# A recurrent attention and two expert layers on one core: the u, k, r diagonal of the first eight units formed in unit layout

## The chip, the core and the metric

The program runs on one core of one Trainium2 chip. The metric is the device time of one execution in microseconds; the three runs of the kernel before took 944.08, 945.52 and 947.94 us.

## What is computed

```
# r, k, v, w: [4, 8, 768, 48] (batch, head, token, channel); u: [8, 48]
for t in range(768):
    cur = einsum('bhd,bhe->bhde', u * k_t, v_t)
    y_t = einsum('bhd,bhde->bhe', r_t, state + cur)
    state = w_t[..., None] * state + einsum('bhd,bhe->bhde', k_t, v_t)
x = y as [3072, 384]
h = x @ w_in;  x = (max(h, 0) + alpha * min(h, 0)) @ w_out     # d_ff = 2048
h = x @ w2_in; out = (h * clip(h + 3, 0, 6) / 6) @ w2_out
```

The change touches one term: the share of a token in its own output, which is the sum over the channels of u, k and r, times v. It stands on the diagonal of a 128 x 128 matrix of weights between tokens.

## The kernel before, in words

**Units.** Each of the four batches of 768 tokens is cut into thirds of 256 tokens (12 thirds t), and the eight heads into four pairs, so there are 48 units n = 4t + pair. A unit's load `un` (L368) holds k, r and w of 256 tokens with 48 channels of one head on partitions 0 to 47 and of the other on 64 to 111. DVE makes two scans of products of w (scan_t L386, scan_g L402, with two small steps between, L394 and L399), POOL or DVE multiplies k and r by them (kr, L423), and PE multiplies k by r for two chunks of 128 tokens and two heads into `A` (function pa, L477) and transposes k (L484). ACT copies that transpose to `kT` (L509), PE multiplies it by v (KV, L516 and L520), DVE carries the state Y on, and ACT spreads Y into block matrices (state, L538).

**The diagonal.** X is a tile of four 128 x 128 matrices, one per head and chunk. ACT writes each as the identity times one number per partition (diag, L458, four activations), and DVE then copies the upper triangle of A over it (triangle, L494 or L499). X and the state matrices give the output y on PE (pc, L588 to L599). ACT writes its upper part (L635, the tile xt, or x for the fourth pair), DVE the rest (L641). The fourth pair's x goes out by six small transfers on SP (spread, L651).

**Where the numbers of the diagonal come from.** They are formed per third in token layout: `add_third` loads for each of two chunks r and k with tokens on partitions (rk, L328), multiplies them by one another and by u_sb (L332, two products, POOL or DVE), and sums them over the channels of each head on DVE (L339) into `p`. u_sb is loaded at the start (L292).

**The experts.** Both layers go by 6 blocks of 512 tokens and 16 slots of 128 columns. A slot is nine matmuls into h (L765 to L767), an activation and a product that split the result in two parts, and nine matmuls into three accumulators. Weight tiles come as 64-bit words (wraw, L729) and pass ACT (L95), DVE (L98, L103), ACT (L738) and DVE or POOL (L742).

**What sets the order.** Class `Plan` (L117) takes every step with the engines that it may run on, a cost for each, a due time and its dependencies, simulates a list schedule by these costs, and the program is then written out engine by engine in the resulting order. Each engine runs its instructions strictly in that order. SP issues all loads and stores. Steps that are marked `pair` are kept from running on POOL and DVE at the same time. Before the first expert matmul the planner fills PE with warming matmuls (L682). Units 0 to 7 are `early`: they use tiles that the experts need later, and every second one has its A in two banks of the accumulators; the others share one A.

Of the kernel before, what the change touches and what calls it, by code (L numbers as in the profile page):

```python
# [7 lines left out]
F32 = mybir.dt.float32  # L8
# [6 lines left out]
AF = mybir.ActivationFunctionType  # L15
ALU = mybir.AluOpType
# [4 lines left out]
P = 128  # L21
B, H, S, D = 4, 8, 768, 48
NPAIR = 4
C = 128
TH = 256
NTH = 12
NT = B * S
DM = H * D
# [3 lines left out]
PR = 112  # L32
# [6 lines left out]
AHEAD = 8  # L39
# [6 lines left out]
def rwkv_moe_moe2(  # L46
# [13 lines left out]
    nc = tc.nc  # L60
    keep = ctx.enter_context(tc.tile_pool(name="keep", bufs=1))
    dram = ctx.enter_context(tc.tile_pool(name="dram", bufs=1, space=DRAM))
    flag = keep.tile([1, 1], I32, name="flag")
    alp = keep.tile([P, NF], F32, name="alp")
    x2d = dram.tile([NB, NK, P, TB], F32, name="x2d")

    with ExitStack() as es:
        fast_path(es, tc, unit, tok, vch, ub, w1, w2, alpha, out, flag, alp, x2d)
# [161 lines left out]
def fast_path(es, tc, unit, tok, vch, ub, w1, w2, alpha, out, flag, alp, x2d):  # L230
    nc = tc.nc
# [18 lines left out]
    u_sb = const.tile([P, DM], F32, name="u_sb")  # L250
    nal = const.tile([P, NF], F32, name="nal")
# [11 lines left out]
    def setup():  # L263
# [8 lines left out]
        nc.vector.memset(ones, 1.0)  # L272
        nc.vector.memset(three, 3.0)
# [18 lines left out]
    o_u = plan.op({"SP": 0.6}, -38.5, lambda e: nc.sync.dma_start(u_sb, ub))  # L292
# [18 lines left out]
    def add_third(t):  # L311
# [7 lines left out]
        v_op[t] = plan.op({"SP": 1.12}, due + 2, load_v, new=[vb]), vb  # L319
        pb = plan.buf("p", 2)  # L320
# [33 lines left out]
    def add_unit(n):  # L354
# [6 lines left out]
        vb, (reds, pb) = v_op[t][1], p_op[t]  # L361
# [91 lines left out]
        def diag(e):  # L453
            pool, tag, nb = (mp, "g", 3) if early else (ap_, "X", 2)
            X = u["X"] = pool.tile([P, 4, C], F32, tag=tag, bufs=nb, name=f"X{n}")
            pp = p_t[t][:, pr].rearrange("p h c -> p (h c)")
            for i in range(4):
                nc.scalar.activation(X[:, i], ident, AF.Copy, scale=pp[:, i : i + 1])  # L458

        o_x = plan.op({"ACT": 1.18}, d - 1, diag, reds, new=[xb], use=[pb])  # L460
# [4 lines left out]
        def pa(e):  # L465
# [17 lines left out]
            for c in range(nkv):  # L483
                nc.tensor.transpose(  # L484
                    T[:, c, :], kr[:, 0, c * C : (c + 1) * C], ident[0:PR, 0:PR]
                )

        o_pa = plan.op({"PE": 0.89 + 0.1 * nkv}, d - 2, pa, o_kr, new=abufs, use=[krb])
# [18 lines left out]
        def kt(e):  # L507
            u["kT"] = ap_.tile([P, 2, PR], F32, tag="kT", bufs=2, name=f"kT{n}")
            nc.scalar.activation(u["kT"][:, 0:nkv, :], u["Tp"][:, 0:nkv, :], AF.Copy)  # L509

        o_kt = plan.op({"ACT": 0.26}, d + 0.5, kt, [o_pa], new=[ktb], use=abufs)
# [684 lines left out]
```

## Time and profile before

| what | us |
|---|---|
| median of 3 runs | 945.52 |
| lowest, highest | 944.08, 947.94 |
| the profiled execution | 945.74 |
| its span, first to last instruction | 944.0 |
| PE busy | 920.3 (97%) |
| DVE busy | 556.3 (59%) |
| ACT busy | 530.9 (56%) |
| POOL busy | 132.3 (14%) |

The busy share is an average over the whole span. The program has a start, in which the early units run and the first weights are prepared, a middle, in which units and slots alternate, and a long end of slots alone; what a microsecond of an engine is worth differs between them, so the stretches have to be read apart. A row of the trace gives the start and the length of an instruction, or of several merged ones with their count; records of neighbouring instructions of an engine may overlap a little.

### The profile page before, as it was taken

The page shows a single profiled execution, that of the slowest core. Times are in us where ns is not written, and L with a number is a line of the kernel's source. Part 1 is how long each engine was busy: PE and PEld are TensorE (multiplying, and loading weights), DVE is VectorE, ACT ScalarE, POOL GpSimd, SP SyncE. Part 2 cuts the span into 40 slices and gives each one's busy share as a digit, 9 for nine tenths or more (in the row PEclk, how much of TensorE's full clock was granted, in tenths as well). Part 3 has the DMA queues.
Part 4 walks back from the last instruction along what each step waited for, and adds up shares of the span by engine and source line. Part 5 has one row for each costly group of instructions (what it writes and reads, how often), then busy time and mean ns, then how long its engine had stood idle before and what let it go on. Part 6 is the DMA issues. An engine that isn't in the chain of part 4 may idle for free.

```text
span 944.0 us, 13745 instructions
## 1 busy us (share of the span) xinstructions
PE 920.3 (97%) x4914; PEld 743.2 (79%) x4914; DVE 556.3 (59%) x1087; ACT 530.9 (56%) x1266; POOL 132.3 (14%) x132
## 2 busy tenths in 40 slices
PE   7899989999999999999999999999999999999996
PEld 5677767878888788878888888888888888888885
DVE  8999997465655645564369886353353443443432
ACT  5998776565656655665378876363353453443331
POOL 4333234021121201100011130000000000000000
PEclk9999999999999999999999999999999999999998
DMA  8888214122312310110056530060140320500001
GB/s 250 256 268 283 81 52 145 55 79 70 107 64 57 109 55 31 58 64 7 9 186 197 175 111 1 1 200 1 54 147 1 123 79 1 172 30 1 34 1 38
DMA packets 36750, 86.20 MB, mean 91 GB/s; under 512 B 5056, under 2 KB 7488, under 8 KB 36672
## 3 DMA queue, kind: packets, MB, share of 16 engines
q1 hardware_dynamic: 36672, 85.22, 28.8%
q8 instruction: 41, 0.67, 0.3%
q14 instruction: 37, 0.30, 0.1%
HBM read 73.41 MB, written 9.44 MB: 88 GB/s over the span
## 4 chain that ended last, share of the span: by engine, by line
PE 82%; DVE 1%; DMA 0%; POOL 0%; issue 0%; POOLq 0%; DVEq 0%
PE acc L765 13%; PE acc L767 13%; PE acc L766 13%; PE h L765 12%; PE h L767 12%; PE h L766 12%; PE A L477 2%; PE y L595 1%; PE y L588 1%; PE A L484 1%; DMA rk<-in_tok 0%; PE y L599 0%; PE A L516 0%; POOL rk L332 0%; PE A L520 0%; DVE rk L332 0%
## 5 line engine op out<-in xcount | busy, mean ns | idle before, releaser
L765 PE MATMUL acc<-g,w 128*128 128x512 f32 x576 | 228.9, 397 | 0.0
L767 PE MATMUL acc<-g,w 128*128 128x512 f32 x576 | 224.6, 390 | 0.0
L766 PE MATMUL acc<-g,w 128*128 128x512 f32 x576 | 224.5, 390 | 0.0
L818 ACT ACTIVATE g<-pg 128x512 fp32r<-128x512 f32 x192 | 120.6, 628 | 137.7 <-PE acc L767 126.8
L821 DVE TENSOR_TENSOR g<-pg,g 128x512 fp32r<-128x512 f32 x176 | 121.7, 691 | 124.8 <-ACT g L818 124.7
L765 PEld LDWEIGHTS acc<-g,w 128*128 128x128 f32 x576 | 108.1, 188 | 23.4 <-issue 0.4
L767 PEld LDWEIGHTS acc<-g,w 128*128 128x128 f32 x576 | 108.1, 188 | 22.8
L766 PEld LDWEIGHTS acc<-g,w 128*128 128x128 f32 x576 | 108.2, 188 | 21.6 <-DVE g L821 0.3
L812 DVE SCALAR_TENSOR_TENSOR pg<-q,h 128x512 f32<-128x512 f32 x96 | 65.9, 686 | 98.6 <-ACT q L803 98.4
L808 DVE SCALAR_TENSOR_TENSOR pg<-h,q 128x512 f32<-128x512 f32 x96 | 66.1, 688 | 96.4 <-ACT q L801 96.3
L803 ACT ACTIVATE q<-h,three 128x512 f32<-128x512 f32 x96 | 65.8, 685 | 100.5 <-PE h L767 100.3
L765 PE MATMUL h<-xt,w 128*128 128x512 f32 x288 | 116.3, 404 | 1.2 <-ACT w L738 1.1
L767 PE MATMUL h<-xt,w 128*128 128x512 f32 x288 | 113.0, 392 | 0.9 <-POOL w L742 0.7
L766 PE MATMUL h<-xt,w 128*128 128x512 f32 x288 | 112.3, 390 | 0.0
L765 PE MATMUL h<-x,w 128*128 128x512 f32 x288 | 112.0, 389 | 0.0
L766 PE MATMUL h<-x,w 128*128 128x512 f32 x288 | 112.0, 389 | 0.0
L767 PE MATMUL h<-x,w 128*128 128x512 f32 x288 | 112.0, 389 | 0.0
L801 ACT ACTIVATE q<-h,nal 128x512 f32<-128x512 f32 x96 | 65.6, 684 | 73.6 <-PE h L767 71.7
L423 POOL TENSOR_TENSOR kr<-un,tg 112x512 f32<-112x512 f32 (+1 forms) x43 | 43.6, 1016 | 225.5 <-PE y L588 207.3
L765 PEld LDWEIGHTS h<-xt,w 128*128 128x128 f32 x288 | 54.9, 191 | 13.3 <-ACT w L738 2.2
L767 PEld LDWEIGHTS h<-xt,w 128*128 128x128 f32 x288 | 54.0, 188 | 14.1 <-DVE w L742 1.4
L766 PEld LDWEIGHTS h<-x,w 128*128 128x128 f32 x288 | 54.1, 188 | 11.3
(93 smaller groups left out, 1262.7 us busy)
## 6 DMA issues: line engine op xcount, KB each, us to landing
wraw<-in_w SPq DMA_DIRECT2D x64, 384.0 KB, 3.7
un<-in_unit SPq DMA_DIRECT2D x48, 337.3 KB, 3.2
raw<-in_w SPq DMA_DIRECT2D x32, 384.0 KB, 3.9
rk<-in_tok SPq DMA_DIRECT2D x24, 384.0 KB, 4.0
v<-in_vch SPq DMA_DIRECT2D x12, 384.0 KB, 3.1
x2d<-st SPq DMA_DIRECT2D x18, 256.0 KB, 2.1
x2r<-x2d SPq DMA_DIRECT2D x18, 256.0 KB, 4.6
out<-st SPq DMA_DIRECT2D x18, 256.0 KB, 3.5
```

The lines of the kernel that those rows point to most:

```text
L423: eng[e].tensor_tensor(out=u["kr"][:, i].rearrange("p a (c s) -> p a c s", c=2), in0=u["in"][:, 0 : 2 * TH].rearrange("p (a c s) -> p a c ...
L477: nc.tensor.matmul(A[h][:, cs], kr[r0 : r0 + D, 0, cs], kr[r0 : r0 + D, 1, cs], start=True, stop=True,)
L484: nc.tensor.transpose(T[:, c, :], kr[:, 0, c * C : (c + 1) * C], ident[0:PR, 0:PR])
L765: nc.tensor.matmul(ps, whi, xhi, start=start, stop=False, skip_group_check=True)
L766: nc.tensor.matmul(ps, whi, xlo, start=False, stop=False, skip_group_check=True)
L767: nc.tensor.matmul(ps, wlo, xhi, start=False, stop=stop, skip_group_check=True)
L801: nc.scalar.activation(q, k["h"], AF.Relu, scale=nal[:, f : f + 1])
L803: nc.scalar.activation(q, k["h"], AF.Relu, bias=three)
L808: nc.vector.scalar_tensor_tensor(out=p, in0=k["h"], scalar=0.0, in1=k["q"], op0=ALU.max, op1=ALU.subtract)
L812: nc.vector.scalar_tensor_tensor(out=p, in0=k["q"], scalar=6.0, in1=k["h"], op0=ALU.min, op1=ALU.mult)
L818: nc.scalar.activation(k["g"][:, 0], k["p"], AF.Copy)
L821: eng[e].tensor_tensor(out=k["g"][:, 1], in0=k["p"], in1=k["g"][:, 0].bitcast(F32), op=ALU.subtract)
```

## The change

For t = 0 and 1 (units 0 to 7) `add_third` returns after the load of v: no token loads, products or sums. Instead each early unit forms z = k u r in its own layout, by one scalar_tensor_tensor on DVE over 256 columns (weigh), with u as one number per partition (a new tile udt of 112 x 4, loaded first). In pa two matmuls more multiply z, chunk by chunk, by a matrix `heads` of 112 x 2 with ones at the rows of each head; their four result columns lie behind the transposes in A. ACT's copy of kT takes these four columns along (228 columns for 224), and diag reads its scales from there, so it now comes after kT of its own unit. The z tiles use the buffers `rk`. The load of u_sb gets a later due time. From t = 2 on all is as before.

```
@@ setup and first loads @@
+        nc.vector.memset(heads, 0.0)
+        nc.vector.memset(heads[0:64, 0:1], 1.0)
+        nc.vector.memset(heads[64:PR, 1:2], 1.0)
...
-    o_u = plan.op({"SP": 0.6}, -38.5, lambda e: nc.sync.dma_start(u_sb, ub))
+    o_ud = plan.op({"SP": 0.5}, -44.0, lambda e: nc.sync.dma_start(udt, ud))
+    o_u = plan.op({"SP": 0.6}, -12.0, lambda e: nc.sync.dma_start(u_sb, ub))
...
@@ add_third @@
         v_op[t] = plan.op({"SP": 1.12}, due + 2, load_v, new=[vb]), vb
+        if t < AHEAD // NPAIR:
+            return
...
@@ add_unit @@
-            pp = p_t[t][:, pr].rearrange("p h c -> p (h c)")
+            if early:
+                pp = u["p"].rearrange("p (c h) -> p h c", h=2)
+            else:
+                pp = p_t[t][:, pr]
             for i in range(4):
-                nc.scalar.activation(X[:, i], ident, AF.Copy, scale=pp[:, i : i + 1])
-
-        o_x = plan.op({"ACT": 1.18}, d - 1, diag, reds, new=[xb], use=[pb])
+                h, c = divmod(i, 2)
+                nc.scalar.activation(X[:, i], ident, AF.Copy, scale=pp[:, h, c : c + 1])
+
+        def weigh(e):
+            z = ap_.tile([P, 2, DM], F32, tag="rk", bufs=2, name=f"z{n}")
+            u["z"] = z[0:PR, 0, 0:TH]
+            eng[e].scalar_tensor_tensor(
+                out=u["z"], in0=u["in"][:, 0:TH], scalar=udt[:, pr : pr + 1],
+                in1=u["in"][:, TH : 2 * TH], op0=ALU.mult, op1=ALU.mult,
+            )
+
+        if early:
+            zb = plan.buf("rk", 2)
+            o_z = plan.op(
+                {"DVE": 0.35}, d - 2, weigh, [o_load, o_ud], new=[zb], use=[ub_], pair=True
+            )
+            o_kr.append(o_z)
+        else:
+            reds, pb = p_op[t]
+            o_x = plan.op({"ACT": 1.18}, d - 1, diag, reds, new=[xb], use=[pb])
...
+            if early:
+                for c in range(2):
+                    nc.tensor.matmul(
+                        A[0][:, 2 * (C + PR + c) : 2 * (C + PR + c + 1)],
+                        u["z"][:, c * C : (c + 1) * C], heads, start=True, stop=True,
+                    )
...
+            t2 = ap_.tile([P, 2 * PR + 4], F32, tag="kT", bufs=2, name=f"kT{n}")
+            u["kT"] = t2[:, 0 : 2 * PR].rearrange("p (c d) -> p c d", c=2)
+            u["p"] = t2[:, 2 * PR :]
+            m = 2 * PR + 4 if early else nkv * PR
+            nc.scalar.activation(t2[:, 0:m], u["Ah"][0][:, 2 * C : 2 * C + m], AF.Copy)
...
+            {"ACT": 0.26}, d - 1.2 if early else d + 0.5, kt, [o_pa], new=[ktb], use=abufs
+        if early:
+            o_x = plan.op({"ACT": 1.18}, d - 1, diag, [o_kt], new=[xb], use=[ktb])
```

The planner makes a new order of it. A row below gives the line, the operation, what is written and read (the number behind a name counts tiles) and the shape. First SP, the start of its queue, before (un are unit loads, rk token loads, v the values):

```order
L368 DMA un_142<-in_unit 112x771
L328 DMA rk_147<-in_tok 128x768
L292 DMA u_sb<-in_ub 128x384
L328 DMA rk_158<-in_tok 128x768
L317 DMA v_172<-in_vch 128x768
L368 DMA un_181<-in_unit 112x771
L368 DMA un_197<-in_unit 112x771
L368 DMA un_200<-in_unit 112x771
L328 DMA rk_207<-in_tok 128x768
L328 DMA rk_229<-in_tok 128x768
L317 DMA v_255<-in_vch 128x768
```

and with the change (udt is the new tile, alp is alpha, wraw a weight tile):

```order
L376 DMA un_147<-in_unit 112x771
L297 DMA udt<-in_ud 112x4
L323 DMA v_156<-in_vch 128x768
L376 DMA un_163<-in_unit 112x771
L376 DMA un_175<-in_unit 112x771
L323 DMA v_186<-in_vch 128x768
L376 DMA un_197<-in_unit 112x771
L299 DMA alp<-in_alpha 128x16
L298 DMA u_sb<-in_ub 128x384
L773 DMA wraw_0_0_221<-in_w 128x384
```

All four token loads are gone, units 1 and 2 follow directly on the first v, and u_sb stands behind unit 3. Next ACT from its second check on, before (junk is the check of a unit's load, X a unit's diagonal, sbd a state step, xt an output):

```order
L446 ACTIVATE junk,sum_w<-un_142 112x259
L509 ACTIVATE kT_204<-A_187 128x224
L446 ACTIVATE junk,sum_w<-un_181 112x259
L458 ACTIVATE X_216<-ident,p_194 128x128 x4
L538 ACTIVATE sbd_103<-Y_0_226,tg_162 48x48 x2
L458 ACTIVATE X_249<-ident,p_194 128x128 x4
L458 ACTIVATE X_275<-ident,p_194 128x128 x4
L635 ACTIVATE xt_294,sum_y<-y_264 112x256
L509 ACTIVATE kT_307<-A_0_282 128x224
L446 ACTIVATE junk,sum_w<-un_197 112x259
L458 ACTIVATE X_314<-ident,p_194 128x128 x4
```

and with the change:

```order
L454 ACTIVATE junk,sum_w<-un_163 112x259
L454 ACTIVATE junk,sum_w<-un_175 112x259
L549 ACTIVATE kT_237<-A_199 128x228
L454 ACTIVATE junk,sum_w<-un_197 112x259
L470 ACTIVATE X_245<-ident,kT_237 128x128 x4
L95 ACTIVATE wa_109<-wraw_0_0_221 128x384
L549 ACTIVATE kT_271<-A_0_227 128x228
L582 ACTIVATE sbd_105<-Y_0_274,tg_167 48x48 x2
L470 ACTIVATE X_289<-ident,kT_271 128x128 x4
```

The first three diagonals stood ahead of the second unit's kT; now each stands behind its own unit's kT, the first also behind the check of the fourth unit, and a weight step (wa) comes between the first two units. Last PE around the first expert matmul h, before:

```order
L588 MATMUL y_841<-kr_737,sbd_104 112x128
L588 MATMUL y_841<-kr_737,sbd_105 112x128
L595 MATMUL y_841<-X_677,v_492 48x128
L599 MATMUL y_841<-X_677,v_492 48x128
L595 MATMUL y_841<-X_677,v_492 48x128
L599 MATMUL y_841<-X_677,v_492 48x128
L477 MATMUL A_851<-kr_833 128x128 x4
L484 MATMUL A_851<-ident,kr_833 128x112
L765 MATMUL h_869<-xt_294,w_0_0_673 128x512
```

and with the change, where eight warming matmuls and h follow on the last row:

```order
L505 MATMUL A_787<-kr_762 128x128 x4
L512 MATMUL A_787<-ident,kr_762 128x112
L632 MATMUL y_798<-kr_565,sbd_104 112x128
L632 MATMUL y_798<-kr_565,sbd_105 112x128
L639 MATMUL y_798<-X_743,v_530 48x128
L643 MATMUL y_798<-X_743,v_530 48x128
L639 MATMUL y_798<-X_743,v_530 48x128
L643 MATMUL y_798<-X_743,v_530 48x128
L560 MATMUL A_787<-v_530,kT_808 64x48
L564 MATMUL A_787<-v_530,kT_808 48x48
```

Before, y_841 is the output of unit 9 and A_851 belongs to unit 10; now A_787 belongs to unit 9 and y_798 is the output of unit 8. A of unit 10 and the output of unit 9 follow on the first h. On DVE, from unit 1's scan to x of unit 7, the order has two token products, two sums, two kr of 512 columns, one triangle of 512 columns and one weight product less, and seven z more. On SP the token loads of t = 2 now stand behind the six transfers of unit 3's x, with the loads of units 9 to 11 behind them.

## Rows read from the trace of the kernel before

**Rows 1.** The page, the span in 40 slices of 23.6 us.
```profile
PE   7899989999999999999999999999999999999996
...
DVE  8999997465655645564369886353353443443432
```
**Rows 2.** Busy time by stretches: length, engines (instructions), PEclk, DMA share, GB/s.
```profile
3.00:12.00 9.00, 6.78 (x45) 4.57 (x43) 6.12 (x15) 3.27 (x9) 2.09 (x4) 0.87 1.00 289
11.30:46.00 34.70, 29.02 (x307) 21.75 (x304) 34.46 (x91) 31.76 (x114) 13.67 (x17) 0.97 0.83 252
53.20:160.00 106.80, 101.69 (x597) 76.96 (x595) 99.91 (x205) 83.45 (x219) 35.31 (x31) 1.00 0.55 174
200.00:400.00 200.00, 200.00 (x1220) 160.73 (x1219) 114.18 (x238) 116.36 (x311) 34.41 (x31) 1.00 0.22 68
```
**Rows 3.** Timeline, the end of the start, DVE, SP and PE: start, length, instruction.
```profile
46.99 0.40 DVE L641 TENSOR_TENSOR x<-y,x 112x256 fp32r<-112x256 f32 x1
...
47.42 4.66 SPq L651 DMA_DIRECT2D xt<-x  x6
...
47.23 0.72 PE L477 MATMUL A<-kr 48*128 48x128 f32 x8 [0.20 <-DVE X L499]
...
49.22 0.26 PE L516 MATMUL A<-v,kT 128*64 128x48 f32 x1
...
53.26 0.48 PE L765 MATMUL h<-xt,w 128*128 128x512 f32 x1
```
**Rows 4.** Whom PE waited for, 47 to 200 us: total, times, longest.
```profile
PE A L477 <- DVE fall L394: 1.3, 1, 1.3
PE A L477 <- DVE kr L423: 1.2, 2, 1.0
```
**Rows 5.** Timeline of the start, DVE and ACT; in brackets the idle time before.
```profile
3.93 0.70 DVE L386 TENSOR_TENSOR_SCAN tg<-un,restart 112x258 f32<-112x258 f32 x1 [0.79 <-DMA un<-in_unit]
...
10.82 0.70 DVE L386 TENSOR_TENSOR_SCAN tg<-un,restart 112x258 f32<-112x258 f32 x1 [0.59 <-DMA un<-in_unit]
...
11.30 1.26 ACT L458 ACTIVATE X<-ident,p 128x128 f32<-128x128 f32 x4
...
12.47 0.66 ACT L538 ACTIVATE sbd<-Y,tg 48x48 f32<-48x48 f32 x2
...
45.58 0.38 ACT L635 ACTIVATE x<-y 112x256 fp32r<-112x256 f32 x1
```
**Rows 6.** ACT's groups from 11.25 to 46 us: count, busy us, mean ns, idle before.
```profile
L446 ACT ACTIVATE junk<-un 112x259 bf16<-112x259 f32 x9 | 3.8, 419 | 3.0 <-DMA un<-in_unit 2.9
L95 ACT ACTIVATE wa<-wraw 128x384 uint16<-128x384 uint32 x4 | 2.5, 626 | 0.0
```
**Rows 7.** The tile rk up to 25 us, DVE's sums and products: ns shortest, median, longest.
```profile
L339 DVE TENSOR_REDUCE p<-rk x4: 538/548/553, 7.4 to 22.9; 128x8 f32<-128x384 f32 x4
...
L332 DVE TENSOR_TENSOR rk<-rk x3: 526/541/544, 5.8 to 18.6; 128x384 f32<-128x384 f32 x3
```
**Rows 8.** DVE, timeline at 6.28, then groups from 10.8 to 47.2 us.
```profile
6.28 0.41 DVE L423 TENSOR_TENSOR kr<-un,tg 112x256 f32<-112x256 f32 x1
...
L499 DVE COPY_PREDICATED X<-mask,A 128x512 f32<-128x512 uint8 x5 | 3.6, 722 | 0.0
...
L423 DVE TENSOR_TENSOR kr<-un,tg 112x512 f32<-112x512 f32 x2 | 2.2, 1082 | 0.0
...
L98 DVE SCALAR_TENSOR_TENSOR wb<-wraw,wa 128x384 int32<-128x384 int32 x2 | 1.1, 546 | 0.0
```
**Rows 9.** Whom PE waited for in the whole span: total, times, longest.
```profile
PE A L477 <- DVE kr L423: 4.9, 6, 1.4
```
**Rows 10.** Timeline from 22.2 to 23.4 us, POOL and DVE.
```profile
22.30 0.63 POOL L423 TENSOR_TENSOR kr<-un,tg 112x256 f32<-112x256 f32 x1 [1.13 <-PE A L484]
...
22.40 0.56 DVE L394 TENSOR_SCALAR fall<-tg 112x2 f32<-112x2 f32 x1
...
23.34 0.15 DVE L399 RECIPROCAL gfirst<-fall 112x2 f32<-112x2 f32 x1
```

More of the change, by code (lines that the diff above doesn't have):

```diff
@@ L67, in rwkv_moe_moe2 @@
     with ExitStack() as es:
-        fast_path(es, tc, unit, tok, vch, ub, w1, w2, alpha, out, flag, alp, x2d)
+        fast_path(es, tc, unit, tok, vch, ub, ud, w1, w2, alpha, out, flag, alp, x2d)
     again = nc.values_load(
@@ L227, in run, with fast_path @@
         return seq
-def fast_path(es, tc, unit, tok, vch, ub, w1, w2, alpha, out, flag, alp, x2d):
+def fast_path(es, tc, unit, tok, vch, ub, ud, w1, w2, alpha, out, flag, alp, x2d):
     nc = tc.nc
@@ L250, in fast_path @@
     u_sb = const.tile([P, DM], F32, name="u_sb")
+    udt = const.tile([PR, NPAIR], F32, name="udt")
+    heads = const.tile([PR, 2], F32, name="heads")
     nal = const.tile([P, NF], F32, name="nal")
@@ L360, in add_unit @@
         u = {}
-        vb, (reds, pb) = v_op[t][1], p_op[t]
+        vb = v_op[t][1]
         c0 = pr * 2 * D
@@ L486, in pa @@
                 )
-        o_pa = plan.op({"PE": 0.89 + 0.1 * nkv}, d - 2, pa, o_kr, new=abufs, use=[krb])
+            if early:
[4 more added lines that the diff above has]
+                    )
+        o_pa = plan.op(
+            {"PE": 0.89 + 0.1 * nkv + (0.2 if early else 0.0)}, d - 2, pa, o_kr, new=abufs,
+            use=[krb] + ([zb] if early else []),
+        )
         def triangle(e):
@@ L507, in kt @@
         def kt(e):
-            u["kT"] = ap_.tile([P, 2, PR], F32, tag="kT", bufs=2, name=f"kT{n}")
-            nc.scalar.activation(u["kT"][:, 0:nkv, :], u["Tp"][:, 0:nkv, :], AF.Copy)
-        o_kt = plan.op({"ACT": 0.26}, d + 0.5, kt, [o_pa], new=[ktb], use=abufs)
+            t2 = ap_.tile([P, 2 * PR + 4], F32, tag="kT", bufs=2, name=f"kT{n}")
[3 more added lines that the diff above has]
+            nc.scalar.activation(t2[:, 0:m], u["Ah"][0][:, 2 * C : 2 * C + m], AF.Copy)
+        o_kt = plan.op(
+            {"ACT": 0.26}, d - 1.2 if early else d + 0.5, kt, [o_pa], new=[ktb], use=abufs
+        )
+        if early:
+            o_x = plan.op({"ACT": 1.18}, d - 1, diag, [o_kt], new=[xb], use=[ktb])
         def kv(e):
```

## Prediction

> **What bounds the kernel now.** The page comes first [rows 1]. Its slices show PE at 8 or 9 from the second slice nearly to the end, while DVE stands at 8 or 9 in the first six slices, for three slices near the middle, and otherwise mostly between 3 and 6. The table by stretches gives it in numbers [rows 2]: from 200 to 400 us PE is busy for all 200.00 us, DVE for 114.18. So from there on the end is set by the columns that PE still has to stream, and nothing that gets faster on another engine moves it. What can move it is the start. The first expert matmul begins at 53.26 us [rows 3]; until then PE runs only attention units, each cut up by waits, and 128 warming matmuls that compute nothing. From 53.20 to 160 us PE is busy for 101.69 of 106.80 us [rows 2]; 2.5 us of the waits there are for kr or the small steps of a unit on DVE [rows 4]. I therefore reckon the time as the start of the first h, plus the PE work still owed at that point, plus PE's waits after it.
>
> The start has a chain of its own [rows 3]. DVE writes unit 7's lower half x at 46.99; its six spreading transfers are issued from 47.42 on and hold SP for 4.66 us; 1.2 us after the last issue h begins. These 6.3 us from x to h are not touched. Ahead of x two engines are nearly full: between 11.30 and 46.00 us DVE is busy 34.46 and ACT 31.76 of 34.70 us [rows 2]. Before that neither is: from 3 to 12 us DVE is busy 6.12 and ACT 3.27 of 9.00 us, and the DMA engines are busy throughout at 289 GB/s. So the change has to be costed in two steps, loads first, then ACT and DVE.
>
> **The loads.** Unit 1's scan_t starts at 10.82 us, when its load has landed [rows 5]. Until then the queue has carried units 0 and 1 (0.345 MB each), two token tiles and v (0.393 each) and u_sb (0.197), by their shapes in four-byte numbers: 2.07 MB. In the new SP order only unit 0, 112 x 4 numbers and v stand ahead of unit 1, 1.08 MB with itself. 0.98 MB at 289 GB/s is 3.4 us, so unit 1 can start near 7.4. That is the largest thing the change gives, but ACT does not get it. In ACT's new order the check of unit 3's load stands ahead of the first diagonal. Unit 3 has to wait for the third unit buffer, that is for unit 0's last product. This began at 6.28 on DVE behind a token product [rows 8]; z takes about the place of that, and on POOL the product takes 0.63 [rows 10], so it ends near 6.9. Up to its end 2.17 MB are carried, 0.1 more than up to unit 1 before, so it lands near 11.1, and after the check the first diagonal starts at about 11.5, against 11.30 [rows 5]. It takes 1.26, to 12.8. The next row of ACT is the first step on weight tile 0_0, which has alp and u_sb ahead of it in the queue: 0.6 MB more, 13.2 us. ACT thus stands for 0.4, and begins its full stretch **0.6 us later**, not 3.4 earlier.
>
> **ACT's work up to unit 7's output.** From the first diagonal to the activation that writes x (45.58, [rows 5]) ACT ran 10 diagonals, 13 state steps, 8 checks and 3 first weight steps, besides 8 kT, 8 outputs and 2 weight copies. In the new order it is 8, 14, 6 and 4; the rest is alike. At 1.26 us for a diagonal of four activations, 0.66 for a state step of two, 0.42 for a check (the reading of its accumulator lies under the next) and 0.63 for a weight step [rows 5, 6] this is -2.5 + 0.7 - 0.8 + 0.6 = **-2.0 us**. The diagonals of units 8 and 9 leave the stretch but come later. With the 0.6 of above, unit 7's output and so the first h come **1.4 us earlier**, near 51.9. A kT copy has 4 columns more for 224: nothing.
>
> **DVE's work.** Removed in the first two thirds are 5 products and 4 sums on DVE, 5 x 0.54 + 4 x 0.55 = 4.9 us [rows 7], and 3 products on POOL. Added are 8 z on DVE. The trace has no such form; its bounds are a product of two 112x256 tiles, 0.41 where nothing holds it up, and the integer form with the same three operands on 384 columns, 0.55 [rows 8]. I take 0.41, which has z's columns: DVE saves 4.9 - 3.3 = **1.6 us** (0.5 by the other). Three memsets more lie in the 0.79 us in which DVE waits for unit 0 [rows 5]. Of the 1.6, DVE being busy 99.91 of the 106.80 us from the first h to 160 [rows 2], I let **1.0** shorten PE's 2.5 us of waits on DVE [rows 4]; the bounds are 0 and 1.6.
>
> **PE's work.** Before the first h the old order has A of unit 10 and the output of unit 9; the new one stops at A of unit 9 and the output of unit 8. One A and one output move behind it. In the trace such a pair runs from 47.23 to the KV matmul at 49.22 [rows 3]: **+2.0 us**. The 16 new matmuls, each in two passes as A's four are eight records, have two columns; at A's pace, 0.72 us for eight records of 128 columns [rows 3], they would cost 2.9 us, and at least 0. Ahead of the first h PE has its waits and, in the new order, 20 warming matmuls fewer (108 for 128), so I price them at 0 and keep 2.9 for the upper end. The granted clock is 0.97 between 11.30 and 46.00 and 1.00 later [rows 2]; if less warming lowers it there, it is on matmuls that wait for others anyway.
>
> **The queue.** SP's loads for the third third now stand behind the spreading of unit 3 and wait for the z tiles of units 6 and 7, which lie in their buffers; behind them stand the loads of units 9 to 11. Unit 8's diagonal, the first to need them, now follows unit 7's output on ACT, which covers the landing: 0, or some 3 us if that cover fails (case C).
>
> **The sum**, against the profiled execution of 945.74 us (its span is 944.0): 945.74 - 1.4 + 2.0 - 1.0 = **945.3**, no change that a measurement can tell. I take 0.5% (4.7 us) for what can be told, so faster is below 940.8 and slower above 950.2. The median of the runs, 945.52, is 0.2 below the profiled one, less than any term here.
>
> **The rivals.**
> *A: DVE, not ACT, sets unit 7's output.* For it: 34.46 of 34.70 us busy, the fuller of the two [rows 2]. Then the 3.4 us of earlier loading count. From unit 1's scan to x DVE has in the new order two products, two sums, two kr of 512 columns, one large copy_predicated and one weight product less, and 7 z more: -1.1 - 1.1 - 2.2 - 0.7 - 0.5 + 2.9 = -2.7 (the weight product at the 0.55 of the weight step, [rows 7, 8]). First h comes 3.4 + 2.7 = 6.1 earlier: 945.74 - 6.1 + 2.0 - 1.0 = **940.6**. Against it: each output passes ACT before DVE, and ACT's order holds the two waits for loads.
>
> *B: the chain inside a unit becomes the bound, and it is slower.* Made of token sums, diagonals could run ahead of their unit: the old order has two in one go on ACT, before the kT of either. Now each waits for kr, PE's A and the kT copy of its own unit, and the triangle waits for it. Where ACT has nothing else meanwhile, 1.25 us are exposed per unit, for units 1 to 7. From four on it decides: 945.3 + 5.0 = 950.3; all seven give **954.1**. For it: PE waits for kr before A in six places, 4.9 us in all [rows 9]. Against it: in the new order a state step, a check or an output stands between a kT and its diagonal.
>
> *C: the change does not do at the start what it says.* The loads before ACT's first diagonals, or those of the third third, come later than reckoned, the first h stays where it was, and a pair is owed: 945.74 + 2.0 = **947.7**. For it: the two waits on ACT; against it: the queue moved 289 GB/s in the same stretch.
>
> *D: z and POOL collide.* A DVE threshold on 112x2 takes 0.56 us beside a POOL kr and ends with it; a like step takes 0.15 alone [rows 10]. The engines hold each other up, and eight z of 0.41, each ahead of a kr on POOL, would put 3.3 us into the units: 945.3 + 3.3 = **948.6**. Against it: POOL is busy 13.67 of 34.70 us [rows 2] and loses three products. The Trainium skill, "SBUF — State Buffer", where it lays out the two physically separate sides, has the rule that speaks against the change here: a DVE instruction with two SBUF inputs and a POOL instruction that reads SBUF contend for one port pair, and the second "fully blocks". The threshold's 0.56 agrees with such a lock.
>
> **How the numbers follow.** Forecast 0.56, A 0.20, B 0.10, C 0.08, D 0.06. Faster: a little over half of A, which lies just past the line, 0.12. Slower: most of B and a trace of C and D, 0.09. Same: 0.79. The forecast's own bounds are 944.7 (all of DVE's 1.6 kept) and 949.2 (none kept, the new matmuls in full). The range reaches down to 940.0 for about half of A and up to 949.5 for C and D; the far half of A and nearly all of B, 2 in 10, are left out.
>
> **What would show it.** Right: unit 1's scan near 7.4, the first diagonal near 11.5, the first h near 52 with one A and one output between it and the next h, z at 0.41, PE's waits from 60 to 160 us about 1 us shorter. Wrong: first h below 49 (A); ACT idle ahead of most diagonals and first h after 55 (B); ACT standing for unit 3 or the weight tile past 14 us (C); POOL's kr well over the 0.63 us of [rows 10] beside z (D). The forecast falls altogether if PE's waits after the first h change by more than 3 us, which no term of the sum does.

## The result: slower by 0.5%, and the profile after

The changed kernel takes 951.49 us (median of 5 runs, 950.45 to 952.61) against 946.68 of the kernel before in the same session: ratio 1.0051, 95% interval 1.0034 to 1.0069. The forecast was 945.3 us, no change that can be told, with 949.5 as the upper end of its range; measured, the kernel is slower and lies above the range. The profiled execution took 950.45 us with a span of 948.5. In the text below TensorE, VectorE, ScalarE and GpSimd are the PE, DVE, ACT and POOL of the rows.

The loads came nearly as forecast. These are rows of the start of the changed kernel, VectorE and ScalarE, that answer to [rows 5]:

```profile
7.81 0.69 DVE L394 TENSOR_TENSOR_SCAN tg<-un,restart 112x258 f32<-112x258 f32 x1 [1.75 <-DMA un<-in_unit]
...
12.08 0.42 ACT L454 ACTIVATE junk<-un 112x259 bf16<-112x259 f32 x1 [2.20 <-DMA un<-in_unit]
...
12.50 1.26 ACT L470 ACTIVATE X<-ident,kT 128x128 f32<-128x128 f32 x4
14.39 0.64 ACT L95 ACTIVATE wa<-wraw 128x384 uint16<-128x384 uint32 x1 [0.63 <-POOL kr L431]
...
48.66 0.36 ACT L679 ACTIVATE x<-y 112x256 fp32r<-112x256 f32 x1
```

Unit 1's scan is 3.0 us earlier; the first diagonal, behind the check of unit 3, stands at 12.50 (11.5 was reckoned). But unit 7's output is at 48.66 where 45.58 stood, and with it the end of the start moves, which answers to [rows 3]:

```profile
49.58 0.41 DVE L685 TENSOR_TENSOR x<-y,x 112x256 fp32r<-112x256 f32 x1
...
50.02 3.78 SPq L695 DMA_DIRECT2D xt<-x  x6
...
55.30 0.48 PE L809 MATMUL h<-xt,w 128*128 128x512 f32 x1
```

The first h begins at 55.30, 2.0 us later instead of 1.4 earlier. From x to h it is 5.7 us. The stretches of [rows 2], and two more:

```profile
3.00:12.00 9.00, 5.78 (x38) 4.22 (x37) 6.47 (x16) 3.07 (x8) 2.87 (x5) 0.92 1.01 262
11.30:46.00 34.70, 32.67 (x295) 26.12 (x296) 29.54 (x77) 27.56 (x95) 10.23 (x14) 0.77 0.71 221
53.20:160.00 106.80, 100.63 (x607) 76.32 (x607) 102.72 (x206) 83.60 (x222) 45.23 (x31) 1.00 0.47 152
200.00:400.00 200.00, 200.00 (x1217) 160.70 (x1216) 114.65 (x237) 116.61 (x311) 35.47 (x32) 1.00 0.23 71
...
10.00:12.00 2.00, 0.62 (x6) 0.65 (x8) 1.97 (x6) 0.00 (x0) 0.73 (x1) 0.62 1.01 257
12.00:26.00 14.00, 13.92 (x100) 10.98 (x99) 11.93 (x31) 9.36 (x33) 4.26 (x6) 0.50 0.78 239
```

From 11.30 to 46 us VectorE did 4.9 us less work (29.54 for 34.46) and ScalarE 4.2 (27.56 for 31.76). TensorE's granted clock stood at 0.50, the 1.2 GHz level, from 12 to 26 us, after TensorE had done nothing but 0.34 us in 8 to 10 and 0.62 in 10 to 12. At this clock its rows for one unit (A, the transposes, the new matmuls; A took 0.72 in [rows 3]) and z, where z waits, are:

```profile
18.36 1.23 PE L505 MATMUL A<-kr 48*128 48x128 f32 x8
19.52 0.63 PE L512 MATMUL A<-ident,kr 112*128 112x112 f32 x2
19.95 0.88 PE L517 MATMUL A<-heads,z 112*128 112x2 f32 x4
...
20.86 0.48 DVE L475 SCALAR_TENSOR_TENSOR z<-un,udt 112x256 f32<-112x256 f32 x1 [1.37 <-PE A L517]
```

Next VectorE's two largest waits from 12 to 110 us (total, times, longest), where the kernel before has 0.24 us without work in all; then those of TensorE for VectorE from 47 to 200 us, which answers to [rows 4]:

```profile
DVE wb L98 <- ACT wa L95: 3.3, 3, 1.5
DVE z L475 <- PE A L517: 2.6, 3, 1.4
```
```profile
PE A L505 <- DVE kr L431: 2.6, 1, 2.6
PE h L809 <- DVE pg L852: 1.5, 1, 1.5
PE A L505 <- DVE gfirst L407: 1.2, 1, 1.2
PE h L811 <- DVE w L786: 0.8, 1, 0.8
```

These four are 6.1 us where the two of [rows 4] are 2.5; one of them, 1.2 us, ends at 52.50, ahead of the first h. Slot 24 (of 192), behind the last weight copy of the first layer, begins at 186.93 against 181.72, and most of these 5.2 us stay: the span is 4.5 longer. From slot 24 to the end all kernels of this document take 761.2 to 762.9 us, so all but some 1 us of what they differ in is made before it.

### The profile page after: what moved, and what is told of

It is laid out like the page before. It is cut to its first block, busy times and chain, and to the rows that moved or that the text cites. A ratio compares the mean times of both kernels' runs of the same rounds, so it can differ in the third digit from the quotient of the medians.

```text
span 948.5 us, 13762 instructions
## 1 busy us (share of the span) xinstructions
PE 926.0 (98%) x4926; PEld 749.5 (79%) x4926; DVE 557.0 (59%) x1087; ACT 530.9 (56%) x1266; POOL 138.0 (15%) x131
## 4 chain that ended last, share of the span: by engine, by line
PE 82%; DVE 1%; issue 0%; POOL 0%; DMA 0%; POOLq 0%
PE acc L809 13%; PE acc L810 13%; PE acc L811 13%; PE h L809 12%; PE h L811 12%; PE h L810 12%; PE A L505 2%; PE y L639 1%; PE y L632 1%; PE A L512 1%; PE y L643 0%; PE A L560 0%; PE A L564 0%; DMA rk<-in_tok 0%; POOL kr L431 0%
## 5 line engine op out<-in xcount | busy, mean ns | idle before, releaser
L811 PEld LDWEIGHTS acc<-g,w 128*128 128x128 f32 x576 | 108.1, 188 | 23.4 <-DVE w L786 0.6
L809 PEld LDWEIGHTS acc<-g,w 128*128 128x128 f32 x576 | 108.1, 188 | 23.4 <-ACT w L782 0.2
L431 POOL TENSOR_TENSOR kr<-un,tg 112x512 f32<-112x512 f32 (+1 forms) x46 | 49.0, 1065 | 240.2 <-PE y L632 218.0
```

The costliest lines, as they stand in the source:

```text
L431: eng[e].tensor_tensor(out=u["kr"][:, i].rearrange("p a (c s) -> p a c s", c=2), in0=u["in"][:, 0 : 2 * TH].rearrange("p (a c s) -> p a c ...
L809: nc.tensor.matmul(ps, whi, xhi, start=start, stop=False, skip_group_check=True)
L811: nc.tensor.matmul(ps, wlo, xhi, start=False, stop=stop, skip_group_check=True)
```

## The experiments

Labels are shortened to their first two characters; ratios are to the kernel before on the same chip. Theories changed on the way. First the clock (C, or theory 1; theory 2 is the order and the chain within a unit), then VectorE's idle time (V), against "regained behind the first h" (S) and against the frame of the prediction (P); then what the change does (W) against the order in which it is issued (O).

One thing has to be kept in mind with every edit: some are made where the finished order is issued, so that all else stays in its place (`e1`, `e2`, `e4`, `f1`, `f2`, `g1` to `g3`, `h1`, `h6`); the others change the planner's list, and the planner lays out everything anew (`e3`, `f3`, `f4`, `g4`, `h3` to `h5`). A new layout also decides anew which of VectorE and GpSimd takes a step, and how many warming matmuls there are.

**1. Start of the chain, four runs.** `e1` puts 28 warming matmuls between A of unit 0 and of unit 1 in the changed kernel; `e2` leaves out the 18 that the kernel before has there; `e3` puts the changed kernel's A of unit 10 and output of unit 9 ahead of the first h; `e4` is `e1` without the heads matmuls.

```diff
 e1          o["fn"](o["eng"])
+            if o.get("unit") == 0:
+                for _ in range(28):
+                    warm_t["one"]("PE")
 e2
-            o["fn"](o["eng"])
+            cold = (cold or o.get("unit") == 0) and o.get("out_of") != 0
+            if not (cold and "filler" in o):
+                o["fn"](o["eng"])
 e3
-            {"PE": 1.945}, s, h_, [w_ops[m, f, 0]] + x_ops,
+            {"PE": 1.945}, s, h_, [w_ops[m, f, 0]] + x_ops + ([] if s else ahead),
 e4 (on e1)
-            if early:
+            if False:
                 for c in range(2):
                     nc.tensor.matmul(
```

> The changed kernel with 28 warming matmuls more on PE between A of unit 0 and A of unit 1, where its trace shows PE waiting 3.04 us (8.34 to 11.38) and the granted clock at 0.50 from about 11 to 27 us after it. Nothing else moves. Theory 1 (the clock): granted clock 1.0 through the start, A with transposes and diagonal sums of one unit 1.7 us in place of 2.5, the 3.9 us for which ACT waits for PE between 14 and 25 us mostly gone, first h 3 to 4 us earlier (51.5 to 52.5 for 55.3), time 947.5 to 948.5 for 951.5. Theory 2 (the order and the chain within a unit, the clock beside the point): first h stays at 55, time 951 to 952, though the clock is up.

> The kernel before without the 18 warming matmuls that stand on PE between A of unit 0 and the output of unit 0 (7.6 to 13.3 us in its trace). There the clock fell to 0.50 at about 10 and was back at 13. Theory 1 (the clock): it now stays at 0.50 until some time between 18 and 27 us, first h 1.5 to 2.5 us later than 53.3, time 1 to 3 us above the kernel before. Theory 2 (the clock beside the point): first h and time within 0.5 us of the kernel before.

> The changed kernel with A of unit 10 and the output of unit 9 made to stand ahead of the first h again, as before the change. The prediction's account (a pair of 2.0 us that is done after the first h in place of before it is work that PE owes either way): first h 2 to 3 us later than 55.3, time within 1 us of the changed kernel. Rival (the pair between the first and the second h is what costs, since it holds up the slots): time 1.5 to 3 us below the changed kernel.

> The first of these kernels (28 warming matmuls more) without the 16 diagonal sums on PE: they are left out, kT is copied without their four columns, and the early diagonals take their scales from a constant column, so the early units' diagonals hold wrong numbers; the order of every engine is otherwise the same. The rows of the changed kernel show 0.52 us for the four records of one unit at full clock, 4.2 us for eight units. If PE has time to spare there once the clock is up, as the prediction priced it: within 1 us of the first kernel. If they stand in the chain of the units: 2 to 4 us below it, first h as much earlier.

Measured: `e1` 951.84 us (ratio to before 1.0047, 1.0031 to 1.0063), first h 54.43; the clock fell to 0.50 all the same, at 17 us instead of between 10 and 12, behind a wait of TensorE of 1.76 us for kT, so this says little about the clock. `e2` 945.94 (0.9988, 0.9976 to 0.9999). `e3` 951.96 (1.0048, 1.0029 to 1.0066). `e4` 949.20 (1.0025, 1.0009 to 1.0041). The row of `e2`'s first h and, of the kernel before and of `e2`, the first of slot 24:

```profile
56.98 0.47 PE L767 MATMUL h<-xt,w 128*128 128x512 f32 x1
...
182.40 0.48 PE L767 MATMUL h<-xt,w 128*128 128x512 f32 x1
```
```profile
181.72 0.48 PE L765 MATMUL h<-xt,w 128*128 128x512 f32 x1
```

A first h 3.7 us later, at a half clock to about 21 us, is 0.7 late at slot 24 and 0.1 at the end of the span. So the start of the first h does not by itself set the end, which the prediction was built on, and in the order of before a half clock at the start does not cost 5 us either. In `e3` the first h came 4.4 later (59.67) than in the changed kernel with nothing owed, for the same time within the intervals; but it is also a new layout (115 warming matmuls for 108), so it shows less. `e4` is 2.1 us below `e1` by the ratios and its first h 1.5 earlier (52.91): the lower end of what the second expectation asks, though the intervals overlap.

**2. Causes one at a time, and the change in halves.** `f1` gives z a ring of its own, since z shares the two buffers of rk and waits for the heads matmuls of two units before (the row at 20.86). `f2` fills TensorE's gaps from 8 to 27 us. `f3` and `f4` apply the change to units 4 to 7 or 0 to 3 alone, each in a new layout (`zed` for `early` where z, heads and the diagonal's source are chosen).

```diff
 f1
-            z = ap_.tile([P, 2, DM], F32, tag="rk", bufs=2, name=f"z{n}")
-            u["z"] = z[0:PR, 0, 0:TH]
+            u["z"] = ap_.tile([PR, TH], F32, tag="z", bufs=3, name=f"z{n}")
 f2
+FILL = {('A', 0): 28, ('KV', 0): 22, ('KV', 1): 8, ('A', 2): 6, ('A', 3): 6, ('y', 1): 6, ('KV', 3): 14}
...
+            for _ in range(FILL.get(o.get("fill"), 0)):
+                warm_t["one"]("PE")
 f3 (f4: ZT = (0,))
+ZT = (1,)
...
+        zed = t in ZT
```

> The changed kernel, with the order of every engine as it is, but z in a ring of three buffers of its own instead of the two that it shares with the weights and token tiles. In the trace of the changed kernel VectorE waits 2.6 us in 12 to 56 us for the matmuls with heads of two units before, which read the buffer that z is to go into. Theory V (the loss is VectorE's time without work before about 110 us, 8 us where the kernel before has 0.3): these waits go, and the time falls by 1 to 2.6 us, to 949 to 950.5. Rival S (what happens before the first h is regained, as in the run without warming; the loss is made after it, by the new order): within 1 us of the changed kernel.

> The changed kernel with 90 warming matmuls put into TensorE's gaps from 8 to 27 us (28 behind A of unit 0, 22 behind its KV, 8 behind KV of unit 1, 6 each behind A of units 2 and 3 and behind the output of unit 1, 14 behind KV of unit 3), nothing else moved. If the granted clock stays at 1.00 to 28 us, theory C (the half clock is the loss: kT, z and the outputs wait for matmuls that take 1.7 times as long) expects the first h 2 to 3 us earlier, at 52 to 53, and 947 to 949 us; theory V expects the part of VectorE's idle time that comes from it, 1 to 2 us; rival S expects the first h earlier and the time within 1 us of the changed kernel.

> Part alone: only units 4 to 7 get their diagonal from z; units 0 to 3 from token rows as in the kernel before, with those loads back in their place. The start of the chain is the one of before, so TensorE's clock and ScalarE's first diagonal at about 11.3 us too. Theory V: VectorE has next to no idle time before 110 us, first h at 52.5 to 53.5, and 945.5 to 947.5 us, as before. Rival S (the new matmuls, z and the new order cost wherever they stand): 949 to 950.5 us.

> Part alone, the other half: only units 0 to 3 get their diagonal from z, units 4 to 7 from token rows. Theory V: the start of the chain is that of the changed kernel (no token load ahead, but clock 0.50 and diagonals behind kT), so most of the loss is here, 949.5 to 951.5 us. Rival S: half of it, 949 us.

Measured: `f1` 950.49 us (1.0038, 1.0022 to 1.0054), not to be told from the changed kernel: the waits for L517 are gone, but VectorE now waits 2.4 us at another place, and its idle time from 12 to 110 us is 8.11 us for 8.14. `f2` 954.83 (1.0082, 1.0062 to 1.0101): the clock held,

```profile
8.00:28.00 20.00, 20.00 (x214) 16.70 (x212) 17.32 (x47) 12.61 (x46) 5.63 (x8) 1.00 0.91 264
```

but TensorE was then busy for all 20 us, and VectorE waited for it at the states (3.3 us). A full clock bought this way did not help; what it would be worth without the matmuls that hold it, `f2` cannot tell. `f3` 949.92 (1.0038, 1.0014 to 1.0062) and `f4` 950.78 (1.0031, 1.0014 to 1.0048): either half costs nearly as much as the whole. `f3`'s runs spread from 947.58 to 959.96; its profiled execution is one of the slowest, 957.17 us, and there the first h is at 59.40 instead of the 53 expected, though units 0 to 3 do what they do before. That fits neither V nor half a loss each.

**3. Loads on one engine, and a control.** `g1` adds 5 us to VectorE in the kernel before, `g2` 5 us to TensorE, `g3` takes 5.6 us from VectorE in the changed kernel (it leaves out a clamp and a reciprocal in units 9 to 20, so their numbers are others), and `g4` changes one planning cost in the kernel before by 0.02.

```diff
 g1          o["fn"](o["eng"])
+            if o.get("gate", 99) < 9:
+                nc.vector.tensor_tensor(out=spare, in0=u_sb, in1=u_sb, op=ALU.mult)
 g2          wt, xt = W[m, f, 0], xts[j]
+            for _ in range(3 if s < 8 else 0):
+                nc.tensor.matmul(
+                    h, wt[:, 0, 0:P], xt[:, 0, 0], start=True, stop=False, skip_group_check=True
+                )
 g3      def floor(e):
+            if 9 <= n <= 20:
+                return
...
         def recip(e):
+            if 9 <= n <= 20:
+                return
 g4
-        o_x = plan.op({"ACT": 1.18}, d - 1, diag, reds, new=[xb], use=[pb])
+        o_x = plan.op({"ACT": 1.2}, d - 1, diag, reds, new=[xb], use=[pb])
```

> The kernel before with 5 us more for VectorE: behind the gate of each of slots 0 to 8 (about 55 to 92 us) one more product of 128 x 384, 0.55 us each, into a tile that nobody reads; the order stays. Theory V (VectorE sets the pace to about 140 us, with 3.1 us of it unused in 110 to 140): the time rises by 1.9 to 5 us, to 948.5 to 952. Theory P (the prediction's frame: the end is the first h plus TensorE's work and its waits, and waits for VectorE in 60 to 160 us are mostly covered): by at most 2 us.

> The kernel before with 5 us more for TensorE at the same place: in each of slots 0 to 7 the first matmul of h is issued three more times ahead of itself, 24 matmuls of 0.21 us; the order stays and the result too. Theory V: TensorE's later waits take it up, the time rises by 0 to 1.5 us. Theory P: what TensorE owes at the first h is what sets the end, the time rises by 4 to 5 us.

> The changed kernel with less for VectorE: in units 9 to 20 the clamp of the product and its reciprocal are left out, 24 instructions of 0.31 and 0.16 us, 5.6 us in about 53 to 165 us (the decays of these units are then divided by other numbers, so the output is not that of the reference); the order stays. Theory V: the time falls by 3 to 5.5 us, to 946 to 948.5, as far as the kernel before. Theory P: by at most 1.5 us.

> A control on the order: the kernel before, with the planner's cost of the four diagonals of a unit at 1.20 instead of 1.18. No work is added or left out; what each engine issues is laid out anew from there. If any new order that the planner makes from this list costs some us (theory O: the loss of the changed kernel is the price of a new order, not of what the change does), 949 to 952 us; if the order is as good as another, within 1.5 us of the kernel before.

Measured against 946.20 of the kernel before: `g1` 949.80 (1.0029, 1.0010 to 1.0048), by the ratio 2.7 of the 5 us arrive; `g2` 947.91 (1.0000, 0.9980 to 1.0021), none, to within 2 us; `g3` 949.84 (1.0030, 1.0010 to 1.0049), some 2 of the 5.6 us are gained on the changed kernel, less than V asks, and the intervals overlap; `g4` **953.37 (1.0067, 1.0045 to 1.0089)**. So 5 us more for TensorE behind the first h do not set the end; VectorE's load counts by about half; and the control, which computes just what the kernel before does, is as slow as the changed kernel. Its layout differs in more than the order: VectorE takes 11 of the products kr instead of 13 and is busy for 559.8 us instead of 556.3 in all, and there are 137 warming matmuls for 128. "Order" stands for all of this from here on. The rows from 12 to 110 and 110 to 140 us, of before, of the changed kernel and of the control (VectorE's busy time is the third behind the length):

```profile
12.00:110.00 98.00, 90.32 (x691) 67.56 (x690) 97.76 (x221) 83.28 (x250) 34.21 (x33) 0.99 0.76 239
110.00:140.00 30.00, 28.11 (x158) 21.37 (x156) 26.91 (x55) 23.67 (x61) 9.33 (x8) 1.00 0.20 57
```
```profile
12.00:110.00 98.00, 91.42 (x678) 70.52 (x676) 89.86 (x201) 80.53 (x243) 35.19 (x31) 0.92 0.70 222
110.00:140.00 30.00, 28.55 (x171) 21.44 (x170) 28.99 (x58) 22.57 (x56) 14.88 (x9) 1.00 0.20 59
```
```profile
12.00:110.00 98.00, 87.23 (x648) 66.18 (x647) 89.30 (x198) 80.32 (x239) 40.68 (x37) 0.95 0.73 233
110.00:140.00 30.00, 25.58 (x145) 19.30 (x144) 29.50 (x57) 20.90 (x50) 8.12 (x6) 1.00 0.20 64
```

The control shows what the changed kernel showed: VectorE idle for 8.70 us before 110 us (8.14 there, 0.24 before), and of the 3.1 us that it has spare in 110 to 140 us before, 0.5 are left (1.0 there). From 12 to 26 us its granted clock is 1.00, so a loss of this size needs no half clock. The last weight copy of the first layer, on ScalarE, in the same three kernels:

```profile
137.85 0.93 ACT L738 ACTIVATE w<-wb 128x384 fp32r<-128x384 f32 x2
```
```profile
146.54 0.52 ACT L782 ACTIVATE w<-wb 128x384 fp32r<-128x384 f32 x1 [0.52 <-DVE wb L103]
```
```profile
146.86 0.51 ACT L738 ACTIVATE w<-wb 128x384 fp32r<-128x384 f32 x1
```

**4. The change in the old order.** `h1` gives the planner the list of the kernel before and issues its order with the token work of units 0 to 7 passed over; z goes behind the first scan of its unit, and a diagonal that would stand ahead of its kT right behind it. z has a ring of its own as in `f1`, and the 128 warming matmuls of before stay. VectorE's order then differs from before by three memsets, the 8 z and the 9 rows taken out. `h3` is a second control on the kernel before; `h4` and `h5` give the two controls' edits to the changed kernel.

```diff
 h1 (in the loop that issues)
+            if "behind" in o and o["behind"] not in done:
+                held[o["behind"]] = o
+                continue
             o["fn"](o["eng"])
+            if "then" in o:
+                o["then"]("DVE")
+            if "kt" in o:
+                done.add(o["kt"])
+                if o["kt"] in held:
+                    held.pop(o["kt"])["fn"]("ACT")
 h3, h5
-        o_tri = plan.op({"DVE": 0.61}, d - 1.5, triangle, [o_kv, o_x], use=abufs + [xb])
+        o_tri = plan.op({"DVE": 0.63}, d - 1.5, triangle, [o_kv, o_x], use=abufs + [xb])
 h4
-            o_x = plan.op({"ACT": 1.18}, d - 1, diag, reds, new=[xb], use=[pb])
+            o_x = plan.op({"ACT": 1.2}, d - 1, diag, reds, new=[xb], use=[pb])
```

> The change's work in the order of the kernel before: the planner gets the list of the kernel before, and when its order is issued, the token loads, products and sums of the first two thirds are passed over, z is issued behind the first scan of its unit, the heads matmuls behind the transposes, and a diagonal that would stand ahead of its kT is put right behind it (VectorE's order then differs from before only by these instructions; z has a ring of its own). Theory O (the loss of the changed kernel is the new order): 1.6 us less for VectorE and 2.0 less for ScalarE in an order that holds, 944 to 947 us, no slower than the kernel before. Theory W (the loss is what the change does: half clock, heads matmuls and kT in the chain): 949 to 952 us.

> A second control: the kernel before with the planner's cost of the masked copy at 0.63 instead of 0.61, no work changed. Theory O: 949 to 954 us as with the first control; theory W: 946 to 948 us (the first control was one bad order).

> The changed kernel with the first control's edit (cost of the diagonals 1.20 instead of 1.18 in both places). Theory O: another order, so another time, 947 to 955 us, and not slower on the whole than the first control's 953.4; theory W: 4 to 6 us above the first control, 957 to 959 us.

> The changed kernel with the second control's edit (cost of the masked copy 0.63). Theory O: within the spread of the orders, 947 to 955 us, and within 3 us of the second control on either side; theory W: 4 to 6 us above the second control.

Measured against 946.29: `h1` **944.54 us (0.9973, 0.9962 to 0.9985)**, faster than both kernels; `h3` 950.84 (1.0041, 1.0025 to 1.0058); `h4` 955.33 (1.0098, 1.0078 to 1.0118); `h5` 954.18 (1.0070, 1.0051 to 1.0090). Theory W is out as the whole cause: the same z, heads matmuls and diagonals behind kT are a gain of 1.7 us in the old order (2.6 by the ratio). Theory O holds: both controls cost 4 to 6 us by their ratios, and compute nothing else than the kernel before. `h1`'s rows of the start, of slot 24 and of VectorE to 110 us:

```profile
9.42 1.26 ACT L477 ACTIVATE X<-ident,kT 128x128 f32<-128x128 f32 x4
...
54.84 0.47 PE L810 MATMUL h<-xt,w 128*128 128x512 f32 x1
...
181.28 0.48 PE L810 MATMUL h<-xt,w 128*128 128x512 f32 x1
```
```profile
12.00:110.00 98.00, 89.18 (x698) 67.50 (x695) 93.60 (x211) 81.49 (x244) 30.77 (x29) 1.00 0.76 227
```

Its first h is as late as in the changed kernel (54.84 and 55.30), yet slot 24 begins 5.6 us sooner; VectorE is idle for 4.4 us to 110 us, not 8.1. The first diagonal is at 9.42, since ScalarE has no check of unit 3 in front of it here, and the clock is 1.00 from 12 us on. With the same edit on both sides, the changed kernel is 3 us behind its control each time (1.0098 to 1.0067, 1.0070 to 1.0041; the intervals overlap): whether the change costs some 3 us in whatever order the planner makes of it, or these orders happen to be the worse ones, cannot be told from these pairs.

**5. One step further.** `h6` is `h1` with z behind the second product of its unit, unit 1's load ahead of v, and unit 1's second scan ahead of unit 0's states.

```diff
+        for first, then in (("load 1", "v 0"), ("scan_g 1", "Y 0 0")):
+            seq.remove(at[first])
+            seq.insert(seq.index(at[then]), at[first])
```

> The change's work in the order of the kernel before, with three pieces moved where token work is gone: z is issued behind the second product of its unit instead of behind the first scan, unit 1's tile is loaded ahead of v, and unit 1's second scan stands ahead of unit 0's new states. Theory O, with VectorE as the engine that sets the pace to about 140 us: the 2.6 us that VectorE waits for tiles and for KV of unit 0 up to 30 us shrink by about 1 us, and 943.5 to 944.5 us against 944.5. Rival R (a small loss at the start is regained behind 110 us, as in the run without warming): no difference to the run in the old order, 944.5 to 945.

Measured: 943.16 us (0.9975, 0.9955 to 0.9996). Against before it is faster; against `h1` the intervals are the same, so whether these moves bring anything stays open.

## Why the prediction was wrong

- **The steps that failed, in the prediction's own terms.** First, "unit 7's output and so the first h come 1.4 us earlier": it came 2.0 later. Second, "I let 1.0 shorten PE's 2.5 us of waits": TensorE's idle time behind the first h grew by 1.3. The pair owed was right. The rows from the first h to slot 24, with the length and TensorE's busy time in front, of before, changed kernel, `h1` and the control `g4`:

```profile
53.26:181.72 128.46, 123.23 (x726) 94.26 (x727) 112.45 (x229) 96.01 (x254) 38.77 (x34) 1.00 0.50 157
55.30:186.93 131.63, 125.10 (x749) 95.62 (x747) 116.83 (x232) 97.89 (x261) 49.41 (x36) 1.00 0.46 147
54.84:181.28 126.44, 122.49 (x726) 94.47 (x727) 113.59 (x231) 97.20 (x254) 42.19 (x34) 1.00 0.51 158
55.15:189.20 134.05, 124.96 (x739) 96.52 (x739) 116.96 (x235) 97.27 (x257) 44.00 (x34) 0.99 0.48 152
```

| against before, us | first h | TensorE's work to slot 24 | its idle time there | slot 24 |
|---|---|---|---|---|
| forecast | -1.4 | +2.0 | -1.0 | -0.4 |
| changed kernel | +2.0 | +1.9 | +1.3 | +5.2 |
| `h1` | +1.6 | -0.7 | -1.3 | -0.4 |
| `g4` | +1.9 | +1.7 | +3.9 | +7.5 |

- **Behind them, the frame**: "I therefore reckon the time as the start of the first h, plus the PE work still owed at that point, plus PE's waits after it." The sum of the three comes out, but they are not independent terms. `e2` had a first h 3.7 us later and no loss, `h1` one 1.6 later and a gain, `g2` 5 us more for TensorE and no loss. Each engine works through a list that is fixed ahead, and what one gains or owes before slot 24 it takes back or loses at waits on the others.
- **The new order was costed by what it moves, not by how well it fits.** The prediction counted the instructions on either side of two points and let the stretch between them shrink by what was saved (ACT's "-2.0 us"). Instead ScalarE's stretch from the first diagonal to x grew from 34.28 to 36.16 us, with 4.2 us less work in 11.30 to 46 us. In the order of before, the same work gained 1.7 us, and two other orders of the old work lost 4.1 and 6.7 thousandths. A hint that was not used may be VectorE's row, 34.46 of 34.70 us [rows 2]: an engine that is idle for 0.24 us of 98 leaves a new order little to gain.
- **"If less warming lowers it there, it is on matmuls that wait for others anyway."** The clock did fall, to 0.50 from 12 to 26 us, and others waited for those matmuls (z 2.6 us, ScalarE's kT copies and outputs). So the price was not 0 at that place. But `e2`, with a half clock to 21 us, lost nothing in the end, `g4` lost as much with a clock of 1.00 from 12 to 26 us, and `f2`, with the full clock, gained nothing. What the clock alone costs in the changed kernel's order stays open.
- **The heads matmuls at 0**: `e4` puts some 2 us on them in the changed kernel's order. In `h1`'s the change gains with them in place; no run leaves them out there. The pace taken for the upper end, 2.9 us, was too fast too: at full clock they are 0.52 us a unit, 4.2 for eight.
- **The loads** were sized well (7.4 against 7.81) but unit 3's landing by 1.0 us and the first weight step by 1.2 too early.
- **z at 0.41** is 0.46 to 0.48 in six of eight, and 0.69 and 0.91 where it began beside a kr on POOL that was already running. The rows, with the kr beside the first of the two:

```profile
4.53 0.64 POOL L431 TENSOR_TENSOR kr<-un,tg 112x256 f32<-112x256 f32 x1 [1.47 <-DVE tg L394]
...
4.77 0.69 DVE L475 SCALAR_TENSOR_TENSOR z<-un,udt 112x256 f32<-112x256 f32 x1
...
33.91 0.91 DVE L475 SCALAR_TENSOR_TENSOR z<-un,udt 112x256 f32<-112x256 f32 x1
```

  So something of rival D is there. The Trainium skill, "SBUF — State Buffer", section "SBUF: two separate sides", says of a VectorE instruction with two SBUF inputs and a POOL one that reads SBUF that the first holds the shared pair for its whole length; these rows agree. But the two z paid 0.7 us together, and two kr that began beside a running z took 0.79 and 0.80 for 0.64; the 3.3 us of D are far off.
- **DVE's 1.6 us, of which 1.0 arrives**: TensorE's waits for VectorE from the first h to slot 24 rose from 2.9 to 5.2 us. That is the wrong way, but within the 3 us by which the text said the forecast falls altogether. By `h1` the saving does arrive, 1.7 us of time for 1.6 of VectorE and 2.0 of ScalarE.
- Of the rivals B came nearest in time and sign, by its mechanism in part: first h came after 55, and from the first diagonal to x ScalarE waited in six places, 4.4 us in all, for TensorE (outputs and kT copies), where it was 0.5 before. But the same chains stand in `h1`, with 3.8 us of such waits, and `h1` gains; so they are not by themselves the loss. The controls without z lose as much.

What stays open is which places of the new order cost most. Nothing that was taken away alone (a wait in `f1`, the half clock in `f2`, the debt in `e3`) brought the time back. What the record does show is a split by order: `e2`, `g2`, `h1` and `h6`, in the order of before, lie at 0.9973 to 1.0000 (and `g1`, with 5 us added, at 1.0029); all eight orders that the planner laid out anew (the changed kernel, `e3`, `f3`, `f4`, `g4`, `h3`, `h4`, `h5`) lie at 1.0031 to 1.0098. Why the order of before is better than all of these is not shown. In the profiles, every kernel that is not slower than before leaves VectorE idle for at most 4.5 us from 12 to 110 us (before 0.24, `h6` 2.36, `g2` 3.65, `h1` 4.40, `e2` 4.46), and every slower one but `g1`, whose 5 us of idle work count alike, for 6.0 or more (`e1` 6.06, `h3` 6.43, the changed kernel 8.14, `g4` 8.70, `h5` 11.59). This goes with the 3.1 us that VectorE has spare later, but it was read off afterwards from one execution each and not tested as a cause. Nor does it rank the losses: `f4` leaves 11.66 us idle and loses 0.31%, `h4` 8.92 and loses 0.98%.

## What to carry to other kernels

Where a planner lays out the order anew, a change is two changes. Run the new work in the old order, and the old work in a new order (one cost moved by a few per cent), before you put the time down to either: here the work was worth -0.27% in the old order, and the new order +0.8%. And where an engine that is not the busiest overall has next to no idle time in the stretch before the steady state, do not count on a new order to fit as well as the old one: here none of eight did.

## What the runs showed of the hardware that was not expected

The granted clock fell to 0.50 where TensorE did next to nothing for a few us, as in 8 to 12 us of the changed kernel (busy for 0.34 and 0.62 us of each two), and was 0.50 from 12 to 26 us although TensorE was busy for 13.92 of the 14.00; 28 warming matmuls moved the fall to 17 us, behind the next wait (1.76 us). Matmuls of two columns are not small: four records of the heads matmuls took 0.52 us at full clock in `e1` and 0.88 at half, where eight of A's 128 columns took 0.71 and 1.23. And a first h that is 3.7 us later, behind some 13 us at the half clock, was worth nothing at the end of a span of 944 us (`e2`).
